# First attention batch of a fused attention and two-MLP kernel: keys loaded in halves, first pair scored from unscaled keys, new order of the whole list

## The chip, the cores and the metric

The kernel runs on one core of a Trainium2 chip. A core has a matrix engine (TensorE, PE in the tables; its weight loads are PEld), VectorE (DVE), ScalarE (ACT), GpSimd (POOL) and SyncE (SP), which here issues the DMAs. The engines run their own instruction lists and wait for each other through semaphores. The metric is the device time of one execution in microseconds (us); lower is better. The kernel before takes 579.96 us, the median of three executions (579.86, 579.96 and 580.83).

## The reference

Three stages follow each other, all in float32. Shapes: q, k, v are (2, 8, 768, 64), that is 2 batches of 8 heads; 1536 tokens of width 512 come out of the attention.

```
# attention: keys near the query, and one summary per block of 32 keys
k_sum = k.reshape(B, H, nb, block, D).max(axis=3)
v_sum = v.reshape(B, H, nb, block, D).mean(axis=3)
scores_l = scale * q @ k.T                      # kept where |i - j| < 16, else -1e9
scores_s = scale * q @ k_sum.T + log(block)
a = softmax(concat([scores_l, scores_s], -1))
x = a @ concat([v, v_sum])
# MLP 1 (gated, 512 -> 1536 -> 512)
xn = x / sqrt(mean(x * x) + 1e-6) * rms_g
x = (silu(xn @ w_gate) * (xn @ w_val)) @ w_out
# MLP 2 (512 -> 2048 -> 512)
h = x @ w_in
out = where(h > 0, h, exp(min(h, 0)) - 1) @ w_out2
```

## The kernel before

A query tile has 64 rows. For it 120 score columns count: 96 keys of the window (`NL`) and the 24 block maxima (`NK - NL`). Two query tiles make a pair and stand on the two halves of the 128 partitions; the eight heads stand as four head pairs, two heads on the two halves of the contraction. So the scores of one pair are two PSUM tiles `s{b}_{j}_{h}` of 128 x (4 head pairs x 120), one for each head of the head pairs, and a pair needs 32 matmuls of 64 x 64 by 64 x 120 and eight runs of exp on ScalarE, one per tile and head pair.

The 1536 tokens are treated in three blocks of 512. The four pairs (eight query tiles) of block 0 come first; nothing else can fill TensorE until their attention is done, so this stretch is a prologue, with `keep_warm` matmuls (line 1296) that compute nothing. From the first projection of the MLP (`pv_0c`, line 764) TensorE has matmuls of 256 or 512 columns. The attention of later pairs, the splitting of weights into a high and a low part (`ws_*`: ScalarE casts the high part, line 135; VectorE subtracts for the low part, line 146) and of activations (`xs*`, lines 141, 735, 744) run beside it on the other engines. Blocks 1 and 2 go through seven products each (`A`, `B`, `C` on lines 1002 and 1180).

In the prologue: the keys of batch 0 arrive as three tiles `kT0_0` to `kT0_2` of 128 x 4 x 256 (line 319 whole, line 325 one half of the head pairs); only `kT0_2` is loaded in two halves. VectorE takes the maxima of 32 keys from each into `ksum0` in six reductions (`max_k`, lines 331 and 335). For each query tile a scaled copy of its keys `ka0_t` is made: 96 near columns from `kT` and 24 far columns from `ksum0` (lines 436 to 441, on ScalarE L141, VectorE L143 or GpSimd L439). Mask and log(32) of a tile are written into PSUM ahead by matmuls from an identity (`premask`, lines 468 to 473), the scores are added to them (`scores_part` for the first pair, line 483; `scores` for the others, line 495), VectorE takes the row maximum (`row_max`, line 506) and ScalarE the exponential with its sum (`exps`, line 513). `guard`, `invert` and `normalize` (lines 519 to 530) finish the softmax, `turn_e` (line 538) transposes it through PSUM, `ats` copies bring it back (line 137 or 135), and `apply_v2` (line 550) multiplies with the values. Pairs after block 0 are masked in a VectorE pass of eight custom instructions instead (`add_mask`, line 502).

The order of all this is not found by a scheduler at run time. `add(engine, cost, due, fn, ...)` records each operation, and `issue` walks a table of numbers `PLAN`; each number names a recorded operation and, where several engines may do it, which. `TAGS` names the PSUM bank of each tile that has a choice:

```
for code in PLAN:
    i, choice = divmod(code, 4)
    engine, _, _, fn, args, _, _, new = self.ops[i]
    for tag, name in new:
        self.tag_of[name] = tag[int(next(picks))] if isinstance(tag, tuple) else tag
    fn(*((list(engine)[choice],) if isinstance(engine, dict) else ()), *args)
```

Costs and due times were the input for finding the table, and have no effect when the kernel runs. What an instruction waits for follows from the tiles that it reads and writes: a matmul into a PSUM tile waits until earlier readers of that tile have finished.

Of the kernel before, what the change touches and what calls it, by code (L numbers as in the profile page):

```python
# [9 lines left out]
F32 = mybir.dt.float32  # L10
# [10 lines left out]
P = 128  # L21
# [30 lines left out]
def fused_kernel(ctx: ExitStack, tc: tile.TileContext, q, k, v, w_gate, w_val, w_out, rms_g, w_in2, w_out2, out):  # L52
# [137 lines left out]
    masks_b = [const.tile([P, NK], BF16, name=f"mask_b{var}") for var in range(2)]  # L190

    def make_mask_b(var):
        m = masks_b[var]
        nc.vector.memset(m[:, NL:], pieces[0])
        nc.vector.tensor_copy(m[:, :NL], masks[1][:, :NL])
        if var == 0:
            nc.vector.memset(m[:QT, :W0], NEG)

    for var in (1, 0, 2):
        add(POOL, {1: 1.5, 0: 0.46, 2: 2.86}[var], 5.0 + var, make_mask, var, r=[] if var == 1 else ["mask1"], w=[f"mask{var}"] + ["sel"] * (var == 2))  # L200
    for var in range(2):
        add(DVE, 0.2, 6.0 + var, make_mask_b, var, r=["mask1"], w=[f"mask_b{var}"])
# [12 lines left out]
    sel = {R: const.tile([P, 32], F32, name=f"sel{R}") for R in (4, 2)}  # L215
    own = const.tile([P, 2 * MT + 30], F32, name="own")

    def make_selectors():
        selector(sel[4], 8, 16, 8, 0)
        selector(sel[2], 0, 8, 16, 0)  # L220
        selector(own, 2 * MT - 2, 2, BLOCK, W0)
# [99 lines left out]
    def load_k_first(b, j):  # L321
        load_k(b, j)

# [3 lines left out]
    def max_k(b, i):  # L327
        j, r = divmod(i, 2)
        if b == 0 and j == NG // 2 - 1:
# [12 lines left out]
    def add_k(b, due, gap):  # L342
        add("-", 0.0, due, take, "ksum", f"ksum{b}", [P, NP, NB], w=[f"ksum{b}"], new=[("ksum", f"ksum{b}")])
        for j in range(NG // 2):
            kt = f"kT{b}_{j}"
            split = b == 0 and j == NG // 2 - 1
# [4 lines left out]
            else:  # L351
                add("SP", 1.4, due - 4 + 1.5 * j, load_k if b else load_k_first, b, j, w=[kt], new=[("x", kt)])
# [8 lines left out]
    def load_vtok(b, R, g):  # L361
        src = (v[b, KB:] if R == 4 else v[b, :KB]).rearrange("(p r) h d -> p r h d", r=R)
        rs = slice(g * R // 2, (g + 1) * R // 2)
        nc.sync.dma_start(out=T[f"vtok{b}_{R}"][:, rs], in_=src[:, rs])

    def mean_v(b, R, first, last, tag):
        pt = new(tag, f"vp{b}", [P, 2, D]) if first else T[f"vp{b}"]
        for r in range(R):
            for g in range(4):
                nc.tensor.matmul(  # L370
                    pt[32 * g:32 * g + 32], sel[R], T[f"vtok{b}_{R}"][:, r, 2 * g:2 * g + 2, :],
# [25 lines left out]
    def add_vsum(b, load, due, tag):  # L397
        vp, vm = f"vp{b}", f"vm{b}"
        for n, R in enumerate((4, 2) if b else (4,)):
            vt = f"vtok{b}_{R}"  # L400
            add("-", 0.0, load, take, "xf", vt, [P, 4, H, D], w=[vt], new=[("xf", vt)])
            for g in range(2):
                add("SP", 0.42 * R, load + 0.1 * n, load_vtok, b, R, g, r=[vt], w=[f"{vt}#{g}"])
# [51 lines left out]
    def far_keys(eng, b, t, r=None):  # L455
        rs = slice(None) if r is None else slice(2 * r, 2 * r + 2)
        key_copy(eng, T[f"ka{b}_{t}"][:, rs, NL:], T[f"ksum{b}"][:, rs])
# [1097 lines left out]
```

## Time and profile before

| | |
|---|---|
| time, median of 3 | 579.96 us (579.86 to 580.83) |
| the profiled execution | 581.04 us, of which the span of its instructions 579.3 us |
| busy in the span | PE 571.3 us (99%), DVE 546.0 (94%), ACT 427.9 (74%), POOL 29.1 (5%) |
| granted TensorE clock | 1.000 throughout, the 2.4 GHz level |
| chain that ended last | PE 95%, DMA 3%, DVE 1% |

The span runs from the first to the last instruction; 1.7 us of the execution lie around it. A line of the profile names the source line, the engine, the operation, and output <- input tiles; "idle before" is how long the engine stood still ahead of the instruction, and what released it. Busy times of pipelined instructions overlap a little, so the distance from one start to the next (the pitch) is what one costs. TensorE is 99% busy, but the share contains the `keep_warm` matmuls of the prologue.

### The profile page before, as it was taken

The page shows a single profiled execution, that of the slowest core. Times are in us where ns is not written, and L with a number is a line of the kernel's source. Part 1 is how long each engine was busy: PE and PEld are TensorE (multiplying, and loading weights), DVE is VectorE, ACT ScalarE, POOL GpSimd, SP SyncE. Part 2 cuts the span into 40 slices and gives each one's busy share as a digit, 9 for nine tenths or more (in the row PEclk, how much of TensorE's full clock was granted, in tenths as well). Part 3 has the DMA queues.
Part 4 walks back from the last instruction along what each step waited for, and adds up shares of the span by engine and source line. Part 5 has one row for each costly group of instructions (what it writes and reads, how often), then busy time and mean ns, then how long its engine had stood idle before and what let it go on. Part 6 is the DMA issues. An engine that isn't in the chain of part 4 may idle for free.

```text
span 579.3 us, 10034 instructions
## 1 busy us (share of the span) xinstructions
PE 571.3 (99%) x3369; PEld 467.8 (81%) x3369; DVE 546.0 (94%) x1156; ACT 427.9 (74%) x954; POOL 29.1 (5%) x77
## 2 busy tenths in 40 slices
PE   8899999999999999999999999999999999999997
PEld 5688788888878888888888888888888888888886
DVE  6999999999989999998799999999999999999992
ACT  5999997989999987653444556586577798879741
POOL 5620100000000000000000000000000000000000
PEclk9999999999999999999999999999999999999999
DMA  8899999989689995125242116342356527065012
GB/s 308 295 338 325 352 335 330 311 284 335 202 261 348 300 345 197 50 82 160 91 153 66 38 42 204 91 137 65 100 161 203 176 89 225 2 193 161 20 52 103
DMA packets 56324, 109.06 MB, mean 188 GB/s; under 512 B 6800, under 2 KB 19600, under 8 KB 56272
## 3 DMA queue, kind: packets, MB, share of 16 engines
q1 hardware_dynamic: 56272, 108.42, 56.4%
q8 instruction: 26, 0.43, 0.3%
q14 instruction: 26, 0.21, 0.1%
HBM read 80.09 MB, written 28.31 MB: 187 GB/s over the span
## 4 chain that ended last, share of the span: by engine, by line
PE 95%; DMA 3%; DVE 1%; issue 0%; POOL 0%; SPq 0%; ACT 0%; ACTq 0%
PE acc L820 14%; PE B_1u L1002 8%; PE ph L764 8%; PE pg L764 6%; PE A_1u L1002 6%; PE C_1u L1002 6%; PE B_2u L1002 6%; PE B_2d L1180 6%; PE B_1d L1180 4%; PE C_2d L1180 4%; PE C_2u L1002 4%; PE A_2u L1002 4%; PE A_2d L1180 4%; PE C_1d L1180 3%; PE A_1d L1180 3%; PE pv L550 2%
## 5 line engine op out<-in xcount | busy, mean ns | idle before, releaser
L1002 PE MATMUL B_1u<-xh,w_1u 128*128 128x512 f32 x144 | 48.4, 390 | 0.0
L764 PE MATMUL ph<-xa,ws_i 128*128 128x512 f32 x192 | 46.1, 392 | 0.0
L764 PEld LDWEIGHTS ph<-xa,ws_i 128*128 128x128 f32 x192 | 35.7, 188 | 7.6 <-issue 0.2
L764 PE MATMUL pg<-xs,ws_g 128*128 128x512 f32 (+1 forms) x168 | 36.3, 364 | 0.0
L1180 PE MATMUL B_2d<-td,wd 128*128 128x512 f32 x144 | 35.1, 389 | 0.0
L135 ACT CAST wd<-rd 128x512 fp32r<-128x512 f32 x49 | 29.7, 619 | 6.9 <-PE B_1d L1180 2.5
L1002 PE MATMUL C_1u<-xh,w_1u 128*128 128x512 f32 x96 | 32.6, 389 | 0.0
L1002 PE MATMUL B_2u<-xh,w_2u 128*128 128x512 f32 x96 | 32.6, 389 | 0.0
L146 DVE TENSOR_TENSOR wd<-rd,wd 128x512 fp32r<-128x512 f32 x49 | 32.5, 681 | 0.0
L1002 PE MATMUL A_1u<-xh,w_1u 128*128 128x512 f32 x96 | 32.5, 389 | 0.0
L1002 PEld LDWEIGHTS B_1u<-xh,w_1u 128*128 128x128 f32 x144 | 27.0, 188 | 6.0 <-ACT B_1u L135 0.3
L764 PEld LDWEIGHTS pg<-xs,ws_g 128*128 128x128 f32 x168 | 27.9, 189 | 4.6 <-issue 0.2
L1180 PEld LDWEIGHTS B_2d<-td,wd 128*128 128x128 f32 x144 | 27.0, 188 | 5.6
L1002 PE MATMUL B_1u<-xl,w_1u 128*128 128x512 f32 x72 | 28.0, 389 | 0.0
L135 ACT COPY h_1u<-B_1u 128x512 f32<-128x512 f32 x19 | 11.1, 590 | 22.6 <-PE B_1u L1002 19.7
L1180 PE MATMUL B_1d<-td,wd 128*128 128x512 f32 x108 | 26.4, 390 | 0.0
L1180 PE MATMUL C_2d<-td,wd 128*128 128x512 f32 x96 | 25.0, 389 | 0.0
L513 ACT ACTIVATE e<-e,nm 128x120 f32<-128x120 f32 x64 | 24.4, 387 | 0.0
L135 ACT CAST td<-z 128x512 fp32r<-128x512 f32 x28 | 17.1, 618 | 9.8 <-DVE z L1163 7.2
L1180 PEld LDWEIGHTS B_1d<-td,wd 128*128 128x128 f32 x108 | 20.2, 188 | 4.4 <-ACT B_1d L135 0.3
L1180 PE MATMUL A_2d<-td,wd 128*128 128x512 f32 x93 | 23.5, 389 | 0.0
L1002 PE MATMUL C_2u<-xh,w_2u 128*128 128x512 f32 x64 | 21.8, 389 | 0.0
(546 smaller groups left out, 1740.9 us busy)
## 6 DMA issues: line engine op xcount, KB each, us to landing
st_i<-in_moe_w_in SPq DMA_DIRECT2D x16, 512.0 KB, 5.7
st_p<-in_moe_w_out SPq DMA_DIRECT2D x16, 512.0 KB, 6.3
st_g<-in_moe_w_gate SPq DMA_DIRECT2D x12, 512.0 KB, 6.3
st_v<-in_moe_w_val SPq DMA_DIRECT2D x12, 512.0 KB, 5.9
st_o<-in_moe_w_out SPq DMA_DIRECT2D x12, 512.0 KB, 6.2
kept_i<-raw_i SPq DMA_DIRECT2D x16, 256.0 KB, 5.9
kept_p<-raw_p SPq DMA_DIRECT2D x16, 256.0 KB, 5.1
va<-in_v SPq DMA_DIRECT2D x17, 192.0 KB, 5.6
```

Source lines behind the costliest of these rows:

```text
L135: nc.scalar.copy(out=out, in_=in_)
L146: (nc.gpsimd if eng == POOL else nc.vector).tensor_sub(out, a, b)
L513: nc.scalar.activation(out=e[:, pr, :], in_=s[:, pr, :], func=AF.Exp, bias=nm[:, pr:pr + 1], scale=1.0 if pre else -1.0, accum_out=ss[:, p ...
L550: nc.tensor.matmul(pv[64 * h:64 * h + 64, pr, n, :], va[:NK, 2 * pr + h, :], T[f"ats{b}_{j}_{h}"][:, pr, QT * n:QT * n + QT], start=True, ...
L764: nc.tensor.matmul(pt[:, i], wt[:, a, kk * P:(kk + 1) * P], xt[:, c, i], start=(kk == 0 and n == 0), stop=(kk == KM - 1 and n == 2))
L820: nc.tensor.matmul(acc, wt[:, a, cs], ot[e], start=(first and n == 0), stop=(last and n == 2))
L1002: nc.tensor.matmul(pt, wt[:, a, cs], xt[e][:, kk], start=first and kk == n == 0, stop=kk == 1 and n == 2, skip_group_check=not first)
L1180: nc.tensor.matmul(pt, wt[:, a, cs], xt[:, e], start=first and n == 0, stop=last and n == 2, skip_group_check=i not in (0, 5))
```

## The change

1. All three key tiles of batch 0 are loaded in halves by head pairs (six DMAs of 256 KB in place of two of 512 KB and two of 256 KB), and each reduction takes one half.
2. The first pair has no scaled key copies. It is scored from `kT0_0` and `ksum0` directly, in two steps of two head pairs: `near_scores` (12 matmuls) and `far_scores` (8). Nothing is written to its PSUM tiles ahead. A VectorE pass `first_mask` (eight custom instructions, line 504) adds `mask_0`, multiplies by the negative scale, writes to SBUF and gives the row's extremum; `first_exps` reads that. The two row maxima and the two `premask` groups of this pair go.
3. One selector tile of 48 columns replaces two; the value tiles for the block means are loaded with rows grouped by two.
4. Costs in the table of operations are adjusted, and `PLAN` and `TAGS` are found anew, so the order changes on every engine.

```
-    masks_b = [const.tile([P, NK], BF16, name=f"mask_b{var}") for var in range(2)]
...
+    def make_mask_0():
+        mask_0 = new("t2", "mask_0", [P, NK])
+        nc.vector.memset(mask_0[:, NL:], log_b / scale)
+        nc.vector.tensor_copy(mask_0[:, :NL], masks[1][:, :NL])
+        nc.vector.memset(mask_0[:QT, :W0], NEG)
...
-        if b == 0 and j == NG // 2 - 1:
+        if b == 0:
             rs = slice(2 * r, 2 * r + 2)
...
-            split = b == 0 and j == NG // 2 - 1
+            split = b == 0
...
+    def first_product(r, n, cols, keys):
+        ts = slice(QT * n, QT * n + QT)
+        for pr in (2 * r, 2 * r + 1):
+            for h in range(2):
+                hs = slice(64 * h, 64 * h + 64)
+                nc.tensor.matmul(
+                    T[f"s0_0_{h}"][ts, pr, cols], T["q0_0"][hs, pr, ts], keys[hs, pr], start=True, stop=True)
+
+    def near_scores(r, tag):
+        if r == 0:
+            for h in range(2):
+                new(tag, f"s0_0_{h}", [P, NP, NK])
+        kt = T["kT0_0"]
+        first_product(r, 0, slice(0, W0), kt[:, :, :W0])
+        first_product(r, 0, slice(W0, NL), kt[:, :, :NL - W0])
+        first_product(r, 1, slice(0, NL), kt[:, :, QT - W0:QT - W0 + NL])
+
+    def far_scores(r):
+        for n in range(2):
+            first_product(r, n, slice(NL, NK), T["ksum0"])
+
+    def first_mask(h, r):
...
+        for pr in (2 * r, 2 * r + 1):
+            nc.vector.tensor_tensor_reduce(
+                T[f"e{n}"][:, pr, :], T[f"s{n}"][:, pr, :], T["mask_0"], -scale, 3.0e38, ALU.add, ALU.min, T[f"nm{n}"][:, pr:pr + 1])
+
+    def first_exps(h, r):
...
+        for pr in (2 * r, 2 * r + 1):
+            e = T[f"e{n}"][:, pr, :]
+            nc.scalar.activation(
+                out=e, in_=e, func=AF.Exp, bias=T[f"nm{n}"][:, pr:pr + 1], scale=-1.0, accum_out=T[f"ss{n}"][:, pr:pr + 1])
...
+            if i == 0:
+                continue
...
-        pre = i < PRE
+        pre = 0 < i < PRE
...
 PLAN = (
...
-    40, 48, 52, 80, 320, 64, 60, 212, 226, 84, 229, 218, 108, 232, 236, 92, 584, 112, 96, 336, 480, 120, 340, 326,
```

Where the new table puts things at three places of the prologue:

SyncE, the first loads of the program, before (`kT` keys, `q` queries by pair, `vtok` values for the block means; a row is one DMA, or two where it says x2):

```order
L325 DMA kT0_2_199<-in_k 128x512
L319 DMA kT0_0_201<-in_k 128x1024
L319 DMA kT0_1_225<-in_k 128x1024
L325 DMA kT0_2_199<-in_k 128x512
L316 DMA q0_0_233<-in_q 128x512
L316 DMA q0_1_304<-in_q 128x512
```

and in the changed kernel:

```order
L324 DMA kT0_1_194<-in_k 128x512 x2
L324 DMA kT0_0_192<-in_k 128x512
L318 DMA q0_0_215<-in_q 128x512
L324 DMA kT0_2_207<-in_k 128x512
L324 DMA kT0_0_192<-in_k 128x512
L324 DMA kT0_2_207<-in_k 128x512
```

The first query tile has moved ahead of three key halves; the last key half is the seventh load of 256 KB in place of the sixth.

VectorE from the maxima of the keys on, before (`ksum` the block maxima, `ka` scaled keys, `nm` row maxima of the score tiles `s`):

```order
L335 TENSOR_REDUCE ksum_237<-kT_0_201 128x4x4 x2
L331 TENSOR_REDUCE ksum_237<-kT_2_199 128x2x8
L335 TENSOR_REDUCE ksum_237<-kT_1_225 128x4x4 x2
L331 TENSOR_REDUCE ksum_237<-kT_2_199 128x2x8
L143 TENSOR_SCALAR ka_1_203<-ksum_237 128x2x24
L143 TENSOR_SCALAR ka_7_299<-kT_1_225 128x4x80
L143 TENSOR_SCALAR ka_7_299<-kT_2_199 128x4x16
L143 TENSOR_SCALAR ka_7_299<-ksum_237 128x4x24
L506 TENSOR_REDUCE nm_0_1_376<-s_0_1_257 128x4
```

and in the changed kernel (the custom instructions of the masking pass stand as ISA, each with a second one that hands over the row's extremum; left out are the second pair of each two, and the four of the other tile):

```order
L330 TENSOR_REDUCE ksum_209<-kT_1_194 128x2x8 x2
L330 TENSOR_REDUCE ksum_209<-kT_0_192 128x2x8
L330 TENSOR_REDUCE ksum_209<-kT_2_207 128x2x8
L330 TENSOR_REDUCE ksum_209<-kT_0_192 128x2x8
L330 TENSOR_REDUCE ksum_209<-kT_2_207 128x2x8
L504 ISA e_0_0_305,nm_0_0_306<-s_0_0_283,mask_200 128x120
L504 ISA nm_0_0_306 128x1
...
L504 ISA e_0_1_341,nm_0_1_342<-s_0_1_284,mask_200 128x120
L504 ISA nm_0_1_342 128x1
...
L143 TENSOR_SCALAR ka_8_368<-kT_1_194 128x4x16
```

The masking pass stands behind all six reductions, two instructions for tile `s0_0_0`, then four for `s0_0_1`, then the last two for `s0_0_0`.

ScalarE from the start to its first exponentials, before:

```order
L141 ACT_TABLE_LOAD
L141 ACTIVATE ka_1_203<-kT_0_201 128x4x96
L141 ACTIVATE ka_0_205<-kT_0_201 128x4x80
L141 ACTIVATE ka_3_228<-kT_0_201 128x4x80
L141 ACTIVATE ka_3_228<-kT_1_225 128x4x16
L141 ACTIVATE ka_6_231<-kT_1_225 128x4x96
L141 ACTIVATE ka_1_203<-ksum_237 128x2x24
L141 ACTIVATE ka_0_205<-ksum_237 128x2x24
L141 ACTIVATE ka_2_241<-ksum_237 128x4x24
L141 ACTIVATE ka_9_293<-kT_2_199 128x4x96
L141 ACTIVATE ka_9_293<-ksum_237 128x4x24
L141 ACTIVATE ka_4_296<-kT_0_201 128x4x16
```

and in the changed kernel:

```order
L141 ACT_TABLE_LOAD
L141 ACTIVATE ka_6_213<-kT_1_194 128x4x96
L141 ACTIVATE ka_2_250<-kT_0_192 128x4x96
L141 ACTIVATE ka_3_252<-kT_0_192 128x4x80
L141 ACTIVATE ka_3_252<-kT_1_194 128x4x16
L141 ACTIVATE ka_4_255<-kT_0_192 128x4x16
L141 ACTIVATE ka_4_255<-kT_1_194 128x4x80
L141 ACTIVATE ka_2_250<-ksum_209 128x4x24
L513 ACTIVATE e_0_0_305,ss_0_0_337<-e_0_0_305,nm_0_0_306 128x120 x2
L513 ACTIVATE e_0_1_341,ss_0_1_379<-e_0_1_341,nm_0_1_342 128x120 x2
```

Twelve key copies stood ahead of the first exponential (the twelfth, `ka_4` from `kT_1`, is not shown); seven do now, and the copies for tile 9 have moved behind the exponentials of four tiles.

## Rows read from the trace of the kernel before

**Rows 1.** The page: the chain of waits that ended last, by engine.

```profile
PE 95%; DMA 3%; DVE 1%; issue 0%; POOL 0%; SPq 0%; ACT 0%; ACTq 0%
```

**Rows 2.** Waits of PE from 33 us to the end: us, times, longest.

```profile
PE pv L550 <- issue: 1.1, 1, 1.1
```

**Rows 3.** Windows: stretch, length, busy us (instructions) PE, PEld, DVE, ACT, POOL; clock, DMA share, GB/s.

```profile
11.60:23.70 12.10, 10.41 (x200) 7.67 (x196) 11.26 (x31) 11.63 (x65) 6.56 (x14) 1.00 0.93 334
23.70:33.40 9.70, 8.48 (x182) 7.15 (x181) 9.70 (x34) 9.01 (x20) 4.01 (x6) 1.00 0.96 310
33.40:47.80 14.40, 14.40 (x97) 13.26 (x96) 13.79 (x44) 14.32 (x44) 5.01 (x7) 1.00 0.87 323
```

**Rows 4.** Timeline of SP: start us, us, engine, line, DMA, count.

```profile
0.79 0.38 SPq L325 DMA_DIRECT2D kT<-in_k  x1
1.23 0.89 SPq L319 DMA_DIRECT2D kT<-in_k  x2
2.17 0.43 SPq L325 DMA_DIRECT2D kT<-in_k  x1
2.64 2.22 SPq L316 DMA_DIRECT2D q<-in_q  x4
```

**Rows 5.** Lines 325, 319 and 316 in 0 to 5 us: from issue to landing.

```profile
DMA to landing us min/median/max: 2.7/4.4/6.0
...
DMA to landing us min/median/max: 5.0/5.4/5.8
...
DMA to landing us min/median/max: 6.2/6.5/6.6
```

**Rows 6.** Timeline of DVE: maxima of the keys, and the pitch of a masking pass [idle before].

```profile
6.24 1.28 DVE L335 TENSOR_REDUCE ksum<-kT 128x16 f32<-128x512 f32 x2 [2.90 <-DMA kT<-in_k]
...
9.21 0.68 DVE L331 TENSOR_REDUCE ksum<-kT 128x16 f32<-128x512 f32 x1
...
28.11 0.26 DVE L502 CUSTOM_DVE_ANT_0 e<-s,mask 128x120 f32<-128x120 f32 x1
...
28.31 0.27 DVE L502 CUSTOM_DVE_ANT_0 e<-s,mask 128x120 f32<-128x120 f32 x1
```

**Rows 7.** Timeline of ACT, from its start to the end of the exponentials.

```profile
0.78 1.28 ACT L141 ACT_TABLE_LOAD   x1 [0.78 <-PEq L1543]
...
6.24 1.97 ACT L141 ACTIVATE ka<-kT 128x384 f32<-128x384 f32 x5 [4.17 <-DMA kT<-in_k]
...
11.62 0.36 ACT L513 ACTIVATE e<-s,nm 128x120 f32<-128x120 f32 x1 [0.19 <-DVE nm L506]
...
23.39 0.39 ACT L513 ACTIVATE e<-s,nm 128x120 f32<-128x120 f32 x1
```

**Rows 8.** Timeline of PE: scores of the first pair, and the start of the projections.

```profile
9.81 1.05 PE L483 MATMUL s<-ka,q 64*64 64x120 f32 x32
...
32.98 0.45 PE L550 MATMUL pv<-ats,va 120*64 120x64 f32 x8 [1.07 <-issue]
33.36 1.69 PE L764 MATMUL pv_0c<-xs,ws_v 128*128 128x256 f32 x12
34.89 2.99 PE L764 MATMUL pg<-xs,ws_g 128*128 128x256 f32 x18
```

**Rows 9.** DVE by line, 0 to 40 us: operation, count | busy us, mean ns | idle before.

```profile
L506 DVE TENSOR_REDUCE nm<-s 128x4 f32<-128x480 f32 x8 | 4.9, 640 | 0.2 <-PE s L495 0.2
L744 DVE SCALAR_TENSOR_TENSOR xs<-xT,g_sb,xs 128x256 fp32r<-128x256 f32 x8 | 3.7, 496 | 0.0
L137 DVE COPY ats<-at 120x512 f32<-120x512 f32 x5 | 3.4, 679 | 0.0
...
L530 DVE TENSOR_TENSOR e<-e,rs 128x480 f32<-128x480 f32 x2 | 1.6, 776 | 0.0
...
L137 DVE COPY va<-va 24x512 f32<-24x512 f32 x2 | 0.8, 424 | 0.1
L270 DVE TENSOR_SCALAR raw_g<-st_g 128x512 uint32<-128x512 uint32 x2 | 0.8, 418 | 0.0
```

**Rows 10.** Timeline of DVE: the low part of the first weights.

```profile
31.12 0.67 DVE L146 TENSOR_TENSOR ws_v<-raw_v,ws_v 128x512 fp32r<-128x512 f32 x1
```

More of the change, by code (lines that the diff above doesn't have):

```diff
@@ L351, in add_k @@
             else:
-                add("SP", 1.4, due - 4 + 1.5 * j, load_k if b else load_k_first, b, j, w=[kt], new=[("x", kt)])
+                add("SP", 1.4, due - 4 + 1.5 * j, load_k, b, j, w=[kt], new=[("x", kt)])
             for r in range(2):
@@ L580, in add_pair @@
             near = [f"kT{b}_{x}" for x in range(lo // (2 * P), (hi - 1) // (2 * P) + 1)]
-            if b == 0 and f"kT0_{last}" in near:
-                near = [x for x in near if x != f"kT0_{last}"] + [f"kT0_{last}#{r}" for r in range(2)]
+            if b == 0:
+                near = [f"{x}#{r}" for x in near for r in range(2)]
             ka = f"ka{b}_{t}"
+            if i == 0:
+                continue
             if early:
                 add({POOL: 0.66, DVE: 0.3, ACT: 0.49}, 0, due, near_keys, b, t, r=near, w=[ka + "#n"], new=[(("ka", "act"), ka)])
-                for r, p in enumerate(parts):
-                    x = 1 / len(parts)
-                    add({POOL: 0.16 + 0.1 * x, DVE: 0.1 + 0.1 * x, ACT: 0.2 + 0.09 * x}, 0, due + 0.1, far_keys, b, t, r if x < 1 else None, r=p, w=[ka + f"#f{r}"])
+                add({POOL: 0.26, DVE: 0.2, ACT: 0.29}, 0, due + 0.1, far_keys, b, t, r=far, w=[ka + "#f0"])
             else:
@@ L599, in add_pair @@
             for r in range(2):
[L600 to L601 removed]
+                add(PE, 0.62, due + 0.3 * r, near_scores, r, tags, r=["q0_0", f"kT0_0#{r}"], w=[f"s{n}#n{r}" for n in ns],
+                    new=[] if r else [(tags, f"s{n}") for n in ns])
+                add(PE, 0.35, due + 0.5, far_scores, r, r=["q0_0"] + [f"s{n}#n{r}" for n in ns] + [f"ksum0#{2 * x + r}" for x in range(NG // 2)],
+                    w=[f"s{n}#f{r}" for n in ns])
         else:
@@ L606, in add_pair @@
             at = due + 0.6 * h
-            if pre:
+            if i == 0:
+                for r in range(2):
+                    add(DVE, 0.41, at + 1.4 + r, first_mask, h, r, r=[f"s{n}#n{r}", f"s{n}#f{r}", "mask_0"], w=[f"e{n}#{r}", f"nm{n}#{r}"],
+                        new=[] if r else [("nm", f"nm{n}"), ("e", f"e{n}")])
+                for r in range(2):
+                    add(ACT, 0.76, at + 2 + r, first_exps, h, r, r=[f"nm{n}#{r}", f"e{n}#{r}"] + [f"e{n}#x", f"ss{n}#x"] * r, w=[f"e{n}" if r else f"e{n}#x", f"ss{n}" if r else f"ss{n}#x"],
+                        new=[] if r else [("ss", f"ss{n}")])
+            elif pre:
                 add(DVE, 0.56, at + 1.9, row_max, b, f"{j}_{h}", f"s{n}", r=[f"s{n}"], w=[f"nm{n}"], new=[("nm", f"nm{n}")])
```

81 lines of the change are left out of this document (36 added, 45 removed), and 301 rows, old and new, of the table PLAN.

## The prediction

> **What bounds the kernel now.** I read the chain of waits first: it is TensorE for 95% [rows 1]. Then I asked where TensorE stands still. The list of its waits from 33 us on holds one entry, 1.1 us, just ahead of the first projection; from there to the end nothing makes it wait [rows 2]. The matmuls after that point are the same in number and shape in both kernels, and the last 28 rows of the order are the same on PE, ACT, DVE and SP. So the time can change in two ways only: the first projection, at 33.36 us [rows 8], starts at another time, or the new order makes TensorE wait later. I next read the prologue by windows. VectorE is busy for 11.26 of 12.10 us and then for 9.70 of 9.70 us, ScalarE for 11.63 and 9.01 us, TensorE itself for less than either of its partners in the first stretch, some of it with matmuls that compute nothing [rows 3]. VectorE is the engine without slack: between 11.6 and 33.4 us it has 0.84 us idle. Even after 33.4 us it is busy for 13.79 of 14.40 us. The reader is to see that whatever adds to VectorE before 33 us moves the operands of the first projections, while what is taken off ScalarE or TensorE there has slack to fall into.
>
> **The change, step by step.** All times are those of the profiled execution, 581.04 us with a span of 579.3 us; it is 1.08 us above the median of 579.96 us, and I carry the difference over to the median.
>
> *Loads.* Before, the keys are issued at 0.79, 1.23 (two) and 2.17 us, the queries from 2.64 us on [rows 4], and land after 2.7, 5.0, 5.8 and 6.0 us, the first query tile after 6.2 [rows 5]: at 3.49, 6.23, 7.5, 8.17 and 8.84 us. The new order sends the same bytes in other pieces, so I read the landings off that curve, halfway where a piece ends in the middle of an old one: tile 1 at 3.5 and 4.9, first half of tile 0 at 6.2, first query at 6.9, first half of tile 2 at 7.5, second half of tile 0 at 8.2, second half of tile 2 at 8.85 us. The first key arrives for VectorE 2.7 us earlier than the 6.24 us at which it begins now [rows 6], the last one 0.67 us later, since a query tile has moved ahead of it.
>
> Two more DMAs of 256 KB cost nothing by these rows: the four query loads are issued within 1.6 us and land within about 2 us, 0.65 us apiece, and the two loads of 512 KB (5.0 us after 1.23 and 5.8 us after about 1.7) land 1.3 us apart, the same for each byte. The Trainium skill says otherwise, in "DMA: Bandwidth & Descriptors", sections "Anatomy of one DMA" and "Bandwidth": about 2.0 us of fixed cost for each transfer, and the advice to batch to 1 MiB or more. Paid in full, two more transfers would put the last half 4 us later. The trace shows that cost only once, in the 2.7 us of the first load; behind it the queue hides it.
>
> *Maxima and first exponentials.* A reduction takes 0.64 to 0.68 us. Now the sixth starts at 9.21 and ends at 9.89 us [rows 6]; after the change it waits for the last half and ends at 8.85 + 0.67 = 9.52 us, 0.37 us earlier. The masking pass follows on the same engine at 0.20 us an instruction [rows 6], so the first two heads are ready at about 9.9 us. ScalarE's table load of 1.28 us [rows 7], now done at 2.06 us, stands behind the landing of tile 1 in the new order and ends at about 6.2 us, still ahead of the second half of tile 0 at 8.2 us. The five key copies that need that half come to some 1.6 us (five took 1.97 [rows 7], and these are narrower), plus one far copy: ScalarE is free at 10.0 us. First exponential at 10.0 instead of 11.62 us: 1.6 us earlier.
>
> *The price on VectorE.* The matmuls of the second two head pairs write the PSUM tiles that the mask is reading, so TensorE waits for the second masking instruction (9.9 us), needs 20 matmuls at 0.033 us (32 took 1.05 [rows 8]) and some 0.2 us until the result is seen: 10.75 us. VectorE's third masking instruction is for the other tile and waits for these, and behind it on VectorE queue the key copies of tiles 8 and 11 and the row maxima of every other pair; for those wait all other exponentials. It stands idle for 0.85 us, about what it idles today in all of this stretch (0.84 [rows 3]). The masks end at 12.0 us, the exponentials of pair 0 come in three bursts up to 13.3 us, and all exponentials end at about 22.4 instead of 23.7 us [rows 7].
>
> Then I counted VectorE's list in both orders from the last reduction to the low part of `ws_v0`, which the third matmul of the first projection needs. More: eight masking instructions (8 x 0.20 = 1.6), one `normalize` (0.78), one `va` copy (0.42), one low part `xs` (0.50), one high part `xs` (0.3, no row of its own, taken like the shift below less a quarter), one shift of raw weights (0.42), three small ones (0.3) [rows 6, 9]: 4.3 us. Less: two row maxima (1.28), one `ats` copy (0.68), one combination of raw weights (0.67, as the 512-wide subtraction of rows 10), a narrow key copy (0.2): 2.8 us. Net 1.5 us more, 0.37 us earlier begun, the same idle: `ws_v0` low would end 1.1 us after today's 31.79 us [rows 10], at 32.9. Walking the list from 12.0 us with starts that overlap their predecessors by 0.1 us, as most rows do, gives 31.6 us. Both ends stay in the range; I take 32.3 us, near the middle, since half of the added operations follow each other without a dependence.
>
> *TensorE.* The memset of `va0` on GpSimd stands ahead of the key copies in the new order, so the values are issued earlier, and the wait of 1.07 us [rows 8] is not due to an operand. By the same walk ScalarE's last `ats` copy of this block ends near 30.2 us; 32 value matmuls follow, 1.1 us like the 32 score matmuls [rows 8]. So TensorE could begin the projection at 31.3 us, 2.06 us ahead of 33.36. But two matmuls later it waits for `ws_v0` low. From there VectorE has 16 operations, 6.4 us, up to the last low part that the third projection needs; TensorE has 5.75 us of work up to that matmul (12 + 12 matmuls of 256 columns at 0.13, 33.36 to 34.89 for 12 [rows 8], eight narrow ones, seven of 512). So its dense run begins as if the first projection had started at 32.3 + 0.65 = 32.95 us, against 33.36: 0.4 us gained. With 31.6 us it is 1.1 us, with 32.9 us it is a loss of 0.2. I add 0.1 us for GpSimd, whose shorter list takes less from VectorE, and forecast 0.5 us: 580.5 for a profiled execution, 579.96 - 0.5 = 579.5 us for the median.
>
> *The rest.* The two `premask` groups that go from TensorE and ScalarE's two near and two far copies lie beside the wait for keys and maxima. They save nothing by themselves; the cover is VectorE's chain. The single selector takes four instructions off GpSimd ahead of the keys, where nothing waits for it. `mask_0` is made while VectorE waits 2.9 us for keys [rows 6].
>
> **The rivals.** (A) *The whole start carries through.* If VectorE's list is as short as my lower walk, and its idle after 12 us is nil, `ws_v0` low is there at 31.3 us and 2.06 us are kept: 577.9 us. For it: 0.84 us of idle today that may vanish. Against it: the count of operations.
>
> (B) *The unexplained wait returns.* 1.07 us ahead of the last value matmuls is charged to nothing that the profile shows. If it comes again where TensorE is dense, it takes the 0.5 us and as much again: 580.5 us, no change within what can be told. If it comes ahead of the first projection, VectorE's delay covers it.
>
> (C) *The masking pass parks VectorE: slower.* The place is the third masking instruction. Keys that arrive in sequence leave VectorE waiting in order: a reduction of the last half stands ahead of all masks, then the exchange with TensorE. Each us of delay beyond 0.85 goes straight through 20 us without slack into `ws_v0` low. From masks ending at 12.9 us on, and with the upper count (32.9 + 0.9 = 33.8, plus 0.65), the projection is no earlier than 34.4: +1.1 us or more, and with the same delay in the narrow `xs` chain 1.3: 581.3 us. For it: landings before are uneven, 2.7 us between the first and the second [rows 4, 5]. Against it: 0.9 us more would need a landing at 9.7 us, later than that of any of the first five loads today.
>
> (D) *The change doesn't shorten ScalarE's chain,* since exponentials start early but end bound by the row maxima: then the shift is that of VectorE alone, which is what I forecast anyway.
>
> **How the numbers follow.** The forecast, with D, has 0.53 and spans 578.7 to 580.2 us (1.3 gained to 0.2 lost); A 0.20 at 577.9; B 0.06 at 580.5; C 0.21 at 581.3. A measurement of this kernel can tell about 0.2%, 1.16 us: faster is under 578.8, slower over 581.1. Of the forecast's chance 0.13 lies under 578.8; with A, faster has 0.33. C lies beyond 581.1: slower 0.21. What is left of the forecast and B is no change, 0.46. The range reaches to A's time and short of C's: 577.9 to 581.2, and leaves out about 0.2.
>
> **What would show it.** In the profile of the changed kernel: the first exponential near 10.0 us and the last near 22.4; an idle of 0.85 us on VectorE ahead of the third masking instruction; `ws_v0` low near 32.3 us, and a wait of TensorE for `ws_v` and then for `xs` right after its first two projection matmuls, 1 to 1.6 us in all, and none from 48 us on. The forecast is wrong if TensorE shows no wait on VectorE after its first projection (A), if the first exponential comes after 11 us (C, or the loads), or if waits show up beyond 48 us.

## The result and the profile after

The changed kernel takes 584.04 us (median of four executions, 583.87 to 584.64), the kernel before on the same chip 580.28 us: a ratio of 1.0066 with a 95% interval of [1.0049, 1.0084]. It is slower by 3.8 us, and the forecast was 0.5 us faster. The profiled execution took 584.12 us, with a span of 582.4 us; against the profile of before (581.04 us, itself 0.8 us above its median) that is 3.1 us more.

I first look at the waits of TensorE from 33 us on, which answer to [rows 2]. Columns: us, times, longest.

```profile
PE lice(256, 512, None)_855 L684 <- DVE lice(256, 512, None)_847 L677: 0.4, 1, 0.4
```

One short wait, and none from 48 us on. So the loss lies almost wholly ahead of the first projection, which the timeline of PE shows (it answers to [rows 8]):

```profile
15.61 1.10 PE L525 MATMUL s<-ka,q 64*64 64x120 f32 x36
18.29 1.06 PE L568 MATMUL at<-ident,e 128*120 128x128 f32 x8 [1.58 <-issue]
...
30.76 0.62 PE L568 MATMUL at<-ident,e 128*120 128x128 f32 x4 [1.69 <-DVE ats L137]
31.31 1.15 PE L580 MATMUL pv<-ats,va 120*64 120x64 f32 x32
32.46 1.06 PE L684 MATMUL 0slice(0, 256, None)_751<-ones,)slice(0, 256, None)_677 128*128 128x4 f32 x8
33.45 1.05 PE L525 MATMUL s<-ka,q 64*64 64x120 f32 x32
34.43 1.15 PE L580 MATMUL pv<-ats,va 120*64 120x64 f32 x32
35.51 1.69 PE L800 MATMUL pv_0c<-xs,ws_v 128*128 128x256 f32 x12
```

The first projection starts at 35.51 instead of 33.36 us: 2.15 of the 3.1 us. The stall on "issue" (TensorE waits for nothing that the profile shows) has moved from 31.9 to 16.7 us and grown to 1.58 us. Then TensorE waits 1.69 us for a transposed tile that VectorE copies. The last run of scores at 33.45 us also needs a VectorE mask, which ends at 33.21 us, but TensorE is busy with the matmuls ahead until 33.4 us and loses nothing there. From the projection on another 0.9 us is lost, of which the view of waits names 0.4.

The first loads, on SyncE's timeline, as [rows 4]:

```profile
0.79 1.34 SPq L324 DMA_DIRECT2D kT<-in_k  x3
2.17 0.44 SPq L318 DMA_DIRECT2D q<-in_q  x1
2.65 1.38 SPq L324 DMA_DIRECT2D kT<-in_k  x3
```

and their landings, lines 324 and 318, as [rows 5]:

```profile
DMA to landing us min/median/max: 2.9/5.2/6.4
...
DMA to landing us min/median/max: 5.8/6.6/6.8
```

The last key half is issued at 3.6 us and is there after 6.4 us, at 9.98 us by its own record; the first query at 7.99 us. Then VectorE, as [rows 6] and [rows 10], the idle time before an instruction in brackets:

```profile
8.65 2.04 DVE L330 TENSOR_REDUCE ksum<-kT 128x16 f32<-128x512 f32 x3 [1.88 <-DMA kT<-in_k]
10.60 0.27 DVE L504 CUSTOM_DVE_ANT_0 e<-s,mask 128x120 f32<-128x120 f32 x1
...
12.20 0.28 DVE L504 CUSTOM_DVE_ANT_0 e<-s,mask 128x120 f32<-128x120 f32 x1 [1.11 <-PE s L482]
...
13.22 0.28 DVE L504 CUSTOM_DVE_ANT_0 e<-s,mask 128x120 f32<-128x120 f32 x1
...
35.00 0.68 DVE L146 TENSOR_TENSOR ws_v<-raw_v,ws_v 128x512 fp32r<-128x512 f32 x1
```

and ScalarE, as [rows 7]:

```profile
4.78 1.28 ACT L141 ACT_TABLE_LOAD   x1 [4.78 <-DMA kT<-in_k]
...
9.39 1.53 ACT L141 ACTIVATE ka<-kT 128x384 f32<-128x384 f32 x5 [2.79 <-DMA kT<-in_k]
...
11.00 0.38 ACT L513 ACTIVATE e<-e,nm 128x120 f32<-128x120 f32 x1
...
24.65 0.44 ACT L543 ACTIVATE e<-s,nm 128x120 f32<-128x120 f32 x1
```

The first exponential does come earlier (11.00 against 11.62 us), but the last one ends at 25.1 instead of 23.8 us, and the low part of `ws_v0` at 35.67 instead of 31.79 us. VectorE's timeline from the last reduction to that low part divides the 3.9 us: reductions end 0.8 us later (10.69 against 9.89), its work between is 22.6 instead of 21.0 us, and its idle time 2.35 instead of 0.9 us.

About 0.8 of the 1.6 us of work stand in one instruction that takes longer. One of VectorE's three runs of `normalize` takes 1.44 us; before, the second of two took 0.65 (first line below, from the timeline of before). It runs while GpSimd does two of the same kind from 25.73 to 27.84 us:

```profile
25.69 0.65 DVE L530 TENSOR_TENSOR e<-e,rs 128x480 f32<-128x480 f32 x1
```

```profile
26.92 1.44 DVE L560 TENSOR_TENSOR e<-e,rs 128x480 f32<-128x480 f32 x1
```

```profile
25.73 2.11 POOL L558 TENSOR_TENSOR e<-e,rs 128x480 f32<-128x480 f32 x2 [1.54 <-DVE ss L549]
```

In all nine traces with the new list this instruction stands beside these two and takes 1.43 or 1.44 us; in the nine with the old list none of VectorE's ahead of 40 us takes more than 0.91. That GpSimd holds it up was not tested by itself.

In some executions of the runs below TensorE's granted clock fell below 1 for some 10 us and the time was 2 to 5 us longer; I call the others undisturbed.

### The profile page after: what moved, and what is told of

It reads as the page before. It is cut to its first block, busy times and chain, and to the rows that moved or that the text cites. A ratio compares the mean times of both kernels' runs of the same rounds, so it can differ in the third digit from the quotient of the medians.

```text
span 582.4 us, 10141 instructions
## 1 busy us (share of the span) xinstructions
PE 571.4 (98%) x3411; PEld 468.2 (80%) x3411; DVE 544.3 (93%) x1169; ACT 430.5 (74%) x959; POOL 26.0 (4%) x65
## 4 chain that ended last, share of the span: by engine, by line
PE 94%; DVE 3%; DMA 1%; issue 1%; SPq 0%; ACT 0%; ACTq 0%; DVEq 0%
PE acc L856 13%; PE B_1u L1038 8%; PE ph L800 8%; PE A_1u L1038 6%; PE C_1u L1038 6%; PE B_2d L1216 6%; PE B_2u L1038 6%; PE pg L800 6%; PE B_1d L1216 4%; PE C_2d L1216 4%; PE C_2u L1038 4%; PE A_2u L1038 4%; PE A_2d L1216 4%; PE C_1d L1216 3%; PE A_1d L1216 3%; PE pv L580 1%
## 5 line engine op out<-in xcount | busy, mean ns | idle before, releaser
L1038 PE MATMUL C_2u<-xh,w_2u 128*128 128x512 f32 x64 | 21.8, 389 | 0.0
```

The lines of the kernel that those rows point to most:

```text
L1038: nc.tensor.matmul(pt, wt[:, a, cs], xt[e][:, kk], start=first and kk == n == 0, stop=kk == 1 and n == 2, skip_group_check=not first)
```

## The experiments

The theory: the new list is longer on VectorE and parks it, and VectorE has no slack. Rivals: the loads; TensorE's stall on "issue"; the new treatment of the first pair by itself. In the table "projection" is its start in the profiled execution, "work" and "idle" are VectorE's, between its last reduction and the low part of `ws_v0`. Where disturbed executions carry a median, I name the others.

| run | us, median | ratio, 95% interval | projection | work | idle |
|---|---|---|---|---|---|
| before | 580.3 to 580.7 | 1 | 33.36 | 21.0 | 0.9 |
| after | 584.04 | 1.0066 [1.0049, 1.0084] | 35.51 | 22.6 | 2.35 |
| e1 before, halves | 581.36 | 1.0019 [1.0010, 1.0027] | 33.12 | 21.8 | 1.2 |
| e2 after, two tiles whole | 584.05 | 1.0062 [1.0049, 1.0075] | 37.33 | 22.8 | 2.7 |
| e3 after, query late | 586.58 | 1.0091 [1.0077, 1.0106] | 37.54 | - | - |
| e4 after, stall moved | 583.99 | 1.0067 [1.0047, 1.0087] | 34.45 | 22.8 | 2.0 |
| e5 after, masks moved | 588.08 | 1.0136 [1.0101, 1.0171] | 33.98 | 20.7 | 3.2 |
| e7 after, exchange loosened | 583.21 | 1.0052 [1.0035, 1.0069] | 34.41 | 22.8 | 1.4 |
| e8 new treatment, old list | 581.87 | 1.0031 [1.0011, 1.0050] | 32.30 | 20.6 | 2.2 |
| e10 before, stall moved | 581.70 | 1.0016 [1.0007, 1.0025] | 34.27 | 21.1 | 2.7 |
| e11 before, VectorE padded | 585.01 | 1.0076 [1.0060, 1.0093] | 36.29 | 23.8 | 2.3 |
| e12 new list, old treatment | 587.46 | 1.0123 [1.0099, 1.0146] | 38.58 | - | - |
| e13 as e8, scores early | 581.42 | 1.0027 [1.0007, 1.0047] | 32.37 | 20.6 | 2.4 |
| e14 after, e2 + e4 + e7 | 583.93 | 1.0053 [1.0035, 1.0072] | 34.79 | 22.8 | 2.3 |
| e15 as e13, unparked | 582.21 | 1.0041 [1.0021, 1.0060] | 34.28 | 20.7 | 4.1 |
| e16 as e12, other banks | 585.82 | 1.0097 [1.0078, 1.0117] | 36.07 | 23.0 | 3.7 |
| e17 before, stall moved | 580.66 | 1.0005 [0.9996, 1.0014] | 32.48 | 21.2 | 1.65 |
| e18 before, stall moved | 580.72 | 1.0005 [0.9996, 1.0014] | 31.92 | 21.2 | 1.0 |

### Loads: e1, e2, e3

e1, in the kernel before:

```
     def load_k_first(b, j):
-        load_k(b, j)
+        t = new("x", f"kT{b}_{j}", [P, NP, 2 * P])
+        for r in range(2):
+            nc.sync.dma_start(out=t[:, 2 * r:2 * r + 2], in_=k[b, j, :, 2 * r:2 * r + 2])
```

> The kernel before, with key tiles 0 and 1 of batch 0 also loaded in halves (nothing else changed, order as before). Theory 'splitting': two more DMAs of 256 KB at the cold start cost the queue about 1 us, the last key half lands near 9.2 us in place of 8.2 and VectorE's reductions end 0.9 us later; time 580.8 to 581.3. Rival 'position': halves cost nothing by themselves (as predicted), the keys landed late only because a query tile went ahead of them: last half near 8.2 us, time within 0.3 us of before.

The halves cost 0.8 us here by the medians, 1.1 by the ratio. The last half lands at 8.73 us; with the loads of before it lands between 7.54 and 8.19 us in five traces (before, e10, e11, e17, e18). The Trainium skill ("DMA: Bandwidth & Descriptors", "Anatomy of one DMA") gives about 2.0 us of fixed cost for each transfer, for those that GpSimd issues, while SyncE issues these; paid in turn for two more it would be an estimated 4 us. The trace does not bear that out behind a filled queue. The reductions still end earlier than in before (9.44 against 9.89 us), so the landing is not what costs; VectorE's work behind them is 0.8 us more with the same list, and why stays open. And the table load now stands behind a key:

```profile
5.44 1.28 ACT L141 ACT_TABLE_LOAD   x1 [5.44 <-DMA kT<-in_k]
6.73 1.80 ACT L141 ACTIVATE ka<-kT 128x384 f32<-128x384 f32 x5
```

e2 does the opposite in the changed kernel:

```
     def load_k_part(b, j, r):
+        if j < 2:
+            if r == 0:
+                nc.sync.dma_start(out=T[f"kT{b}_{j}"], in_=k[b, j])
+            return
```

> The changed kernel with key tiles 0 and 1 loaded whole again, at the places of their first halves; all else as changed. 'Splitting': last key half lands near 8.9 in place of 9.98 us, first masking instruction near 9.6 in place of 10.60, time about 1 us less (583.0). 'Position': landing stays near 9.9, time unchanged (584.0). If the wait of TensorE for its own instructions sets the exponentials, the landing moves and the time falls by less than 0.5 us.

Whole tiles bring the table load back to 0.79 us and the last key to 8.14 us, and the time stays: 583.7 us in the two fastest executions, 583.9 in the fastest of after. (Its profile fell into a clock dip, 0.58 in 30 to 35 us, hence the late projection.) So the loads are not what made the changed kernel slow. e3 issues the first query behind the last key half:

```
+        q0 = seq.pop(self.at(seq, "load_q", 0, 0))
+        seq.insert(self.at(seq, "load_k_part", 0, 2, 1) + 1, q0)
```

> The changed kernel with the first query tile issued behind the last key half instead of ahead of three halves. 'Position': last key half near 9.3 us in place of 9.98, but the query at 9.9 in place of 7.99, so that the first scores wait for it: masks no earlier, time 583.9 to 584.5. 'Slow query load' (the 1.9 us between the third and the fourth landing belongs to that load): last half at 8.2 to 8.7 us, time 583.0 to 583.5.

The last half lands at 9.20 us and the query at 9.88, as 'position' had it. Most executions of it were disturbed (the undisturbed one took 584.5 us); of the time it says no more than that this is no improvement.

### The stall on "issue": e4, e10, e17, e18

Around such a stall the trace has a 16 KB transfer on an instruction queue, which ends 1.4 to 1.5 us before the stall does: in after one at 15.77 us that took 1.13 us, in before one at 30.39 us that took 1.09 us. So it is with all twelve such stalls of more than 0.25 us ahead of 60 us, in eleven of the eighteen traces: each ends 1.33 to 1.57 us after a 16 KB transfer does. From the start of the transfer to the stall TensorE had run 52 records of small matmuls and their weight loads in after, 72 in before. The theory is that TensorE runs out of instructions there. Extra small matmuls early would shift where the blocks end; e4 in after, e10 in before:

```
     def keep_warm(i):
...
+        for _ in range(30 if i == 3 else 0):
+            nc.tensor.matmul(pt[:, 0, :16], idle_w, idle_w[:, :16], start=True, stop=True)
```

> The changed kernel with 30 more matmuls of 16 columns that compute nothing, placed where TensorE waits for keys (5.6 to 8.7 us). They only move the later matmuls against the blocks of 16 KB in which TensorE's instructions are fetched. 'Instruction fetch': the 1.58 us ahead of the first transposes at 18.29 us go to under 0.5 us, ScalarE's 1.24 us behind them too, time 582.5 to 583.3. Rival 'other cause' (a semaphore or a slow GpSimd): the wait stays at the same matmul, time 583.8 to 584.3.

> The kernel before with 30 matmuls of 16 columns more among the first keep_warm matmuls, which move the places where TensorE's instruction blocks end. Theory (the 1.07 us stall of 31.91 to 32.98 us that no operand explains is a wait for instructions): the stall is gone from there, the projection starts at 32.4 to 32.8 instead of 33.36 us, 579.3 to 579.8 against 580.3, if no new stall stands in a dense place. Rival (the stall belongs to that matmul whatever comes before): it stays at the same matmul, 580.3.

In e4 the 1.58 us are gone, and a shorter stall stands elsewhere:

```profile
PE at L568 <- DVE ats L137: 1.6, 1, 1.6
PE pv L580 <- issue: 0.6, 1, 0.6
PE lice(256, 512, None)_885 L684 <- DVE lice(256, 512, None)_877 L677: 0.4, 1, 0.4
```

The projection starts 1.06 us earlier, and three of the four undisturbed executions take 583.0 to 583.5 us, the fourth 584.9: the stall is worth up to 1 us of the 3.8. In e10 it moved too, as the theory said, but into two others (1.2 and 1.1 us), so the time that the theory gave did not come, and the 30 matmuls delayed the scores: in before TensorE has matmuls without a gap from 6.3 us to its first scores, and the first exponential came at 12.29 us. e17 and e18 therefore replace wide keep_warm matmuls by narrow ones (98, or 66 with three wide ones left):

```
-        for _ in range(2):
+        for _ in range(0 if i in (3, 4, 0) else 2):
...
+        for _ in range(98 if i == 3 else 0):
+            nc.tensor.matmul(pt[:, 0, :32], idle_w, idle_w[:, :32], start=True, stop=True)
```

> The kernel before with its first six wide keep_warm matmuls (512 columns, 0.42 us each at that point) replaced by 98 of 32 columns, about as long together, so that TensorE's instruction blocks end some 180 instructions earlier than in before, or by the next block some 60 to 70 later. Theory (the stall of 1.07 us at 31.9 us is a block that arrives late, and it goes when the block's end falls among the wide projection matmuls): no wait of TensorE for issue between 25 and 40 us, projection at 32.3 to 32.7 instead of 33.36, 579.6 to 580.0 against 580.4. Rival (VectorE's low parts set the dense start whatever TensorE does): the stall goes, but TensorE waits as much for ws_v0 or xs, 580.4.

> The same with three of the six wide matmuls left and 66 narrow ones, so that the blocks end some 130 instructions earlier (or as many later) than in before. Theory: the third block then ends in the run of scores and transposes of 22 to 28 us, where TensorE waits for others anyway: no stall after 30 us, 579.6 to 580.0. Rival: as for e17, 580.4, or a stall ahead of scores that VectorE waits for, 581.

No stall is left in either, and e18's projection starts 1.44 us earlier than that of before. The time is the same, as the rival had it. Where the gain goes is seen in e18's timeline of PE and in its waits from 33 us on:

```profile
31.92 0.39 PE L764 MATMUL pv_0c<-xs,ws_v 128*128 128x256 f32 x1
32.49 1.58 PE L764 MATMUL pv_0c<-xs,ws_v 128*128 128x256 f32 x11 [0.18 <-DVE xs L744]
```

```profile
PE at L538 <- DVE xT L137: 0.3, 1, 0.3
```

Set side by side matmul by matmul, e18 is 1.44 us ahead of the profile of before at the first projection, 0.86 us ahead from 36 us on, and 0.46 us ahead from 100 us on; the rest is within the scatter between executions. VectorE, which had not become faster, takes the start back. Its own instructions, set side by side in the same way from 40 us on, stand at -0.5 us against before in e18, +0.06 in e17, +0.2 in e1, +1.9 in e15 and +3.75 in e11, and TensorE, whatever its start, has come to -0.46, +0.07, +0.25, +1.9 and +3.8 by 101 us. So the 0.46 us that stayed are those by which VectorE itself was ahead.

### VectorE without slack: e11, e5

e11 puts sixteen multiplications on VectorE ahead of `place_v` in before:

```
     def place_v(eng, b):
+        for _ in range(0 if b else 16):
+            nc.vector.tensor_scalar(pad, pad, 1.0, 0.0, op0=ALU.mult, op1=ALU.add)
```

> The kernel before with sixteen small multiplications on a spare tile (128 x 32) put on VectorE ahead of place_v, at about 18 us; at 0.10 to 0.17 us each they cost VectorE 1.6 to 2.7 us, and nothing reads them. Theory (between 10 and 33 us VectorE has no slack, so work added there moves the projection and the time): ws_v0 low comes later by the whole of it, the projection by that less about 0.5 to 1 us that TensorE stands still today just ahead of it, and the time is 581.5 to 582.5 against 580.7. Rival (TensorE or ScalarE set the projection): ws_v0 low moves, the projection moves by less than 0.3 us, 580.7.

VectorE's timeline has the pad, and the waits of PE from 9 us on what became of it:

```profile
18.91 3.42 DVE L392 TENSOR_SCALAR pad<-pad 128x32 f32<-128x32 f32 x16
```

```profile
PE pv L555 <- DVE ats L137: 3.5, 1, 3.5
```

I had set an instruction at 0.10 to 0.17 us; it takes 0.21, so the pad is 3.42 us. `ws_v0` low comes 4.1 us later, the projection 2.9 us, and the time grows by 4.3 us. All four executions have a clock dip; in the profile it stands in the stretch of the wait. The windows view has it (length, busy us of PE, PEld, DVE, ACT and POOL, then the clock):

```profile
20.00:30.00 10.00, 6.49 (x85) 5.17 (x84) 9.04 (x30) 5.25 (x21) 3.79 (x6) 0.83 0.51 166
```

The dip is part of the price, and the time went past the 582.5 us of the theory. The direction is plain: what is added to VectorE here comes through.

e5 takes some 2 us off VectorE's list ahead of `ws_v0`, in after:

```
+        late = [away("add_mask", 0, "4_1"), away("exps", 0, "4_1"), away("copy_keys", 0, 10), away("add_mask", 0, "4_0")]
+        n = self.at(seq, "split_b", "ws0_g1") + 1
+        seq[n:n] = late
+        s5 = away("scores", 0, 5)
+        seq.insert(self.at(seq, "project", "pg0_1") + 1, s5)
```

> The changed kernel with three VectorE steps of the fifth pair (add_mask 4_1, copy_keys 10, add_mask 4_0: some 2.05 us) and the exps behind them moved behind the second low part; the scores of the sixth pair, which wait for those masks, move behind the second projection product, so TensorE's first projections no longer have these 32 matmuls (1.05 us) in front but in their middle. Theory (VectorE's list ahead of the low part of ws_v0 sets the projection): ws_v0 low at 33.6 instead of 35.7 us, projection at 33.5 to 34.0, and of the 1.5 to 2 us gained 1.05 is paid back for the moved scores unless TensorE waits there anyway: 582.5 to 583.5. Rival (loads, or TensorE's own chain of attention, set the projection): projection stays at 35 us or later, and the time is 584 or, with the scores in a dense place, 585.

The projection starts 1.53 us earlier, as VectorE's list says; but the two undisturbed executions take 585.3 and 586.3 us, not 582.5 to 583.5. The 1.05 us of scores now stand among the projections, and more waits follow:

```profile
PE lice(256, 512, None)_855 L701 <- DVE lice(256, 512, None)_847 L694: 1.3, 1, 1.3
PE s L542 <- DVE nm L549: 0.6, 1, 0.6
```

The work was put off, not removed, and VectorE is as short of time behind the projection as ahead of it.

### The exchange, and after with all three edits: e7, e14

```
+        put(seq.pop(self.at(seq, "near_scores", 1)), "first_mask", 0, 0)
+        put(seq.pop(self.at(seq, "first_mask", 1, 0)), "far_scores", 1)
+        put(seq.pop(self.at(seq, "far_keys", 0, 6)), "first_mask", 1, 1)
```

> The changed kernel with the exchange between mask and scores of the first pair loosened: the near scores of the second two head pairs stand ahead of the first mask, the far scores behind the first two pairs of masks, and one far key copy fills the gap. Theory (the parked VectorE is worth its idle time): the four masking pairs end at 12.7 to 12.9 instead of 13.5 us, VectorE's idle between 10 and 33 us falls from 2.35 to about 1.6 us, ws_v0 low and the projection come 0.7 us earlier, 583.3. Rival (something later, such as the instruction stall or TensorE's transposes, hides it): masks end earlier but the projection stays within 0.2 us of 35.5, 584.

The time is as expected, the reason only in part: the masks end at 13.22, not at 12.8 us, and VectorE's wait for the scores is 0.9 instead of 1.1 us. But the 1.58 us stall is gone from this order as well, though no instruction was added. I can't part the two.

> The changed kernel with three edits together: tiles 0 and 1 loaded whole (e2), 30 small matmuls early (e4) and the loosened exchange (e7). Theory (these three are worth 0.2, about 1 and about 0.2 us, and the rest of the 3.5 us is the list): 582.4 to 583.0. Rival (stall and exchange are the same microsecond, since e7 lost the stall as well): 583.0 to 583.5.

With whole tiles, a shifted stall and the loosened exchange together, the four executions take 582.4 to 584.8 us, no better than e4 or e7 alone, as the rival had it, though their median lies above its 583.5. That stall and exchange are largely the same microsecond fits this, but is not shown: a stall of 0.7 us on "issue" is back in this order. VectorE's work stays at 22.8 us.

### Treatment and list apart: e8, e13, e15, e12, e16

e8 is the changed code (tiles 0 and 1 whole) with the order of before, each step of the first pair in the place of the one it replaces.

> The new treatment of the first pair alone: scored from unscaled keys and masked in a VectorE pass, all else in the order of the kernel before, with the key loads of before (tiles 0 and 1 whole). Theory (the new list is what costs, not the treatment): within 0.8 us of before, 579.5 to 581, with ws_v0 low at 31.5 to 32.5 us. Rival (the treatment itself parks VectorE and costs): projection at 34.5 us or later, 582 or more.

e13 moves the 40 score matmuls ahead of a keep_warm and a premask group.

> As e8 (new treatment, old list, old loads), with the 40 score matmuls of the first pair moved ahead of one keep_warm and one premask group on TensorE, so that only the far scores are left when the last reduction ends. Theory (in e8 VectorE waited 1.3 us for TensorE's fillers and scores ahead of its first mask): masks start at 10.0 to 10.4 instead of 11.0 us, VectorE's idle between 10 and 33 us falls below 1.3 us, projection at 31.5 to 32.0, and the time 580.6 to 581.3, level with before. Rival (the late waits of e8, not its prologue, make its time): masks earlier, time 581.5 to 582 as e8.

Both stay within 0.3% of before, though above it, and above the 581.0 and 581.3 us at which their theories ended. VectorE's work is 20.6 us, less than in before; it waits for TensorE instead (e13, DVE from 9 to 34 us), and its idle is 2.4 us where the theory of e13 had less than 1.3:

```profile
DVE nm L540 <- PE s L529: 1.2, 1, 1.2
DVE e L508 <- PE s L486: 0.8, 1, 0.8
```

The projection starts 1 us early, and as in e18 it is given back, 0.7 us of it between 90 and 101 us. So the treatment alone gains nothing, and by the medians costs 0.7 to 1.1 us.

> As e13 (new treatment, old list, old loads), with VectorE unparked: the row maximum of the second pair stands behind the first two heads' masks and the first half of the third, not between them, and TensorE does the second pair's scores right behind the far scores (the keep_warm that stood between comes behind them, a premask group ahead). Theory (the treatment's early exponentials are a real gain, which parks on VectorE and the list's order gave away): VectorE's idle between the last reduction and ws_v0 low falls from 2.4 to about 1.3 us, ws_v0 low at 31.0 to 31.4, the projection at 31.4 to 31.8 us, and the time 579.5 to 580.4, under before's 580.7. Rival (TensorE's instruction stall or a later wait takes the gain): projection within 0.3 us of e13's 32.4 and 580.9 or more.

e15 reorders four steps to unpark VectorE. Its executions split: five take 580.7 to 581.2 us, as e13's better ones, seven 582.0 to 586.2 us. The profile, one of the second kind, shows why its masks start at 12.53 us: TensorE's fillers run at half the pace of e13's. The second pair of wide fillers in the timeline of PE, e13 and then e15:

```profile
6.17 0.59 PE L1342 MATMUL warm<-idle_w 128*128 128x512 bf16 x2
```

```profile
7.45 1.05 PE L1342 MATMUL warm<-idle_w 128*128 128x512 bf16 x2
```

Up to there both have the same order. It is no improvement, and the gain that its theory expected did not come. No version that I ran beats the kernel before.

e12 is the converse, the new list with the old treatment.

> The new order alone: the whole list of the changed kernel with the first pair treated as before (scaled copies of its keys, premask, row maximum) and the keys of tiles 0 and 1 loaded whole. Theory (the new list costs most of the 3.5 us): projection at 34 us or later and 582.5 to 584. Rival (list and treatment cost only together, through the exchange of mask and scores on VectorE): 580.5 to 581.5.

It does not part the two: TensorE waits for PSUM banks that the old treatment holds until the exponentials have read them. e16 gives one of the first pair's score tiles another bank and moves two keep_warm groups ahead.

> As e12 (new list, first pair treated as before), with the first pair's scores in two PSUM banks that nothing else wants early and two keep_warm groups moved ahead of them, so that TensorE no longer waits for the first pair's exponentials to free a bank. Theory (the list puts about 2 us more work on VectorE ahead of the low part of ws_v0, whatever the first pair's treatment): VectorE's work between the last reduction and ws_v0 low is 22.5 to 23.5 us (21.0 before), projection at 34 us or later, 582.3 to 583.5. Rival (the list is only long because of the masking pass): work 21.3 us or less, 581.3 or less.

Work on VectorE is 23.0 us, 2 us more than in before, in a kernel without the masking pass of the first pair. The windows view from the last reduction to the low part of `ws_v0` has it as the third busy time:

```profile
9.50:36.20 26.70, 21.59 (x446) 16.94 (x445) 22.97 (x73) 21.90 (x92) 11.89 (x22) 1.00 0.79 272
```

The undisturbed executions take 584.5 us, 4 us over before and 1.0 us over the upper end of the theory's forecast. Some of its 3.7 us of idle comes from steps that the list places for the other treatment:

```profile
PE s L495 <- POOL ka L439: 1.2, 1, 1.2
...
DVE nm L506 <- PE s L483: 2.4, 1, 2.4
```

So the list, with either treatment, has 1.6 to 2.1 us more of VectorE's work, 0.8 of it in the long `normalize`, and with the old list neither the work nor most of the time is there. How much of e16's time is its work and how much those waits, the runs do not part.

## Why the prediction was wrong, step by step

**Right.** The place: VectorE ahead of `ws_v0`, "the engine without slack" (e11, e5, e16). The count of its list in sum, "Net 1.5 us more", measured 1.6; but that it came so close is in part luck. The one more `normalize` was counted at 0.78 us and cost 1.13, since one of the three takes 1.44 us beside GpSimd, and key copies that fell by 0.55 us where 0.2 was counted made up for it. The 0.1 us that was added because GpSimd "takes less from VectorE" went the other way there. The exchange that parks VectorE ahead of the third mask: 0.85 us forecast, 1.11 measured. The table load: done "at about 6.2 us", measured 6.06. No wait from 48 us on.

**The step that failed** is the sum for `ws_v0` low: 1.5 us more work, "0.37 us earlier begun, the same idle". Work was right; the other two were not. Idle was not "about what it idles today": the wait for the scores came on top, with 0.6 us for a transpose behind the stall and 0.4 for `va`, 2.35 against 0.9 us. The reductions ended 0.8 us later, not 0.37 earlier. So 31.79 + 1.6 + 1.45 + 0.8 = 35.65; measured 35.67, forecast 32.3. Of the forecast's own ends the upper one (32.9) still assumed all this idle away. The walk that gave 31.6 had 19.6 us from the last mask to that low part; measured are 22.2 us, of which 20.9 are work and 1.2 idle.

**Landings.** The last half was put at 8.85 and came at 9.98 us, the first query at 6.9 and came at 7.99. In e4, e5 and e7, whose loads are the same, the last half came at 9.07, 9.51 and 9.74 us. I read landings off one profile to 0.1 us where they scatter by 0.9; e2 shows that this decided little in the end.

**The first exponential** came at 11.00 instead of 10.0 us, since five key copies waited 2.79 us for the second half of tile 0; the gain of 0.6 us that was left did not reach the last one.

**Ahead of the projection.** "TensorE could begin the projection at 31.3 us" and wait behind it. It waited ahead of it: 1.58 us on "issue" at 16.7 us and 1.69 us for a copy on VectorE at 29 us. The prediction treated the 1.07 us of "issue" as a thing that stays or goes at one place (B); it moves with every list.

**Rival C was the right kind**, and its sign: masks from 12.9 us on (measured 13.50), a parked VectorE, the projection past 34.4 us. Its price of 1.3 us was too low, as it took the wait alone and not the lost start, the idle behind the stall and the 0.9 us behind the projection. **Rival A** falls: `ws_v0` low came 4.4 us after its 31.3, and e18 shows that of a start 1.44 us earlier two thirds are given back.

**What stays open.** Of the 0.9 us behind the projection 0.4 is named. How much of e7's gain is the exchange and how much the stall was not parted, nor what the new list would cost without the long `normalize`.

## What to carry to other kernels

Count the list of the engine without slack as work, idle and start, each with its own row, and let no idle of the old order pay for a wait in the new one: a wait adds unless the old idle is shown to have the same cause. Delays and gains are not alike: a delay of the bound engine came through (in e11 3.4 us of pad, 3.8 at the end of the span, a clock dip included), of a gain on another engine two thirds or more were given back within 70 us (e18, e13). What one instruction costs beside a busy neighbour is a row of its own too: 1.44 instead of 0.65 us. A new order for the whole list is a change of its own; test it apart from the edit that it came with (e8 against e16).

## What was not expected of the hardware

- The trace has 16 KB transfers of 0.9 to 1.4 us on an instruction queue (27 in after). In runs of small matmuls TensorE stood still for 0.3 to 1.6 us without an operand to wait for, and each of twelve such stalls ends 1.33 to 1.57 us after one of these transfers; the place moves, or the stall goes, with the number of instructions ahead of it (e4, e10, e17, e18). That TensorE had run out of instructions is the reading that fits; no row says so.
- The table load of ScalarE takes over the wait of the first instruction behind it: 0.78 us in before, 4.78 in after, 5.44 in e1.
- In the first microseconds the same 512-column matmul passes in 0.42 us and later in 0.21 us, the pace of the 1.2 and 2.4 GHz levels, while the granted clock in the rows stands at 1.00. The step came between 4.2 and 5.5 us in e13 and at 10.0 us in e15, with the same matmuls in the same order ahead; TensorE stood still for a key from 4.75 to 5.23 us in the one and from 4.85 to 5.66 us in the other. What decides was not tested.
- With two more transfers on the queue the last landing came 0.5 to 1.2 us later (e1, one trace: 8.73 us; with the loads of before 7.54 to 8.19).
- A VectorE `normalize` of 128 x 480 takes 0.65 us alone, 0.91 where one on GpSimd overlaps it for 0.4 us (before), and 1.44 where one overlaps it for 0.9 us (after).
